# Local and pooled attention with two feed-forward layers on one core: pooled q and k of two pairs of heads as matrix products

## The chip, the cores and the metric

One core of a Trainium2 chip runs the whole program. The metric is the device time of one execution in microseconds (us); the kernel before was run three times, and its median is the figure that changes are compared with.

## The reference

q, k and v are (4, 8, 576, 64): four batches, eight heads, 576 rows. Each head does two attentions and adds them: one on rows averaged by fours (144 pooled rows, its output repeated four times), one on a band of rows less than four apart. Two feed-forward layers follow on all 2304 rows.

```python
q_d = q.reshape(B, H, Sd, factor, D).mean(axis=3)      # factor 4, Sd = 144; k and v alike
out_up = np.repeat(sm_attn(q_d, k_d, v_d), factor, axis=2)
mask = np.abs(pos[:, None] - pos[None, :]) < factor
out_local = softmax(where(mask, scale * q @ k.T, -1e9)) @ v
x = (out_up + out_local), heads side by side: (2304, 512)
h = x @ w_in;  x = (h * sigmoid(h)) @ w_out            # first layer, d_ff = 2048
r = max(x @ w2_in, 0);  out = (s * r * r + b) @ w2_out # second layer
```

## The kernel before

The kernel writes down operations with an engine, a cost, the buffers that they read and write, and a priority (`op`). A planner (`Weave.plan`) walks through them in a modelled time: of the operations that could start first it takes the one with the lowest priority number, gives it to its engine, and so fixes each engine's order. If nothing of high urgency can start on an engine at that moment, the planner puts other work there, such as the splitting of weights. Each engine then executes its own order strictly in that order; the chip's real times change nothing in it. Constants such as `PT0` or `DEC0` are the priorities of the stages. Some operations may go to ScalarE or VectorE (`EITHER`), whichever the planner expects to end first. Where TensorE would idle for more than 0.477 us in the plan at the start, `fill` puts small products on `spin` there.

Heads are worked in pairs, `hq` 0 to 3, so that two heads of 64 fill 128 partitions. For batch 0 the rows of a pair arrive as `nq`, `nk` (96 rows x 6 x 128) and `nv` (`rows`). `b_turn` (L699) transposes q and k by TensorE into `pq`, and copies them to `qkT` (or `qT`, `kT`). `down` does the pooled attention: `pool_rows` adds v by fours (L586, L587), two VectorE reductions (L604, L605) add the turned q and k by fours into `dq` and `dk`, `part` copies `dq` with a factor into the block-diagonal `q_diag`, and then scores `pS` (L634), softmax (L638 to L649, L332), transposes `pT` and the product with v, `pU`, give `upT`. `banded` does the local attention of the pair: `pB` (L748), mask `be` (L756), softmax (L771 to L764), `pBT`, `pBO`, and the sum of both attentions into `xf` (L797).

When a pair's 512 columns of `xf` are done, `x_split` makes `xh` on ScalarE (L541) and the rest `xl` on VectorE (L542). The first layer (`mix1`) multiplies in three products, high by high, low by high, high by low (all at L807), for 16 slices `m` of the weights: `hp`, then `g` (silu, L826), `gh` (L827), `gl` (L828), then `y`. `g` has one buffer and `hp` two: the `hp` of slice m needs `g` of slice m-2, and `g` of slice m needs `gl` of slice m-1. Each block of 512 columns passes through all 16 slices; block 0 starts when the fourth `xl` of batch 0 is there.

Weights arrive as 64-bit numbers and are split on VectorE in four steps a tile: L387, L390, L393, then a cast (L322, either engine) and L397. Both halves stay in SBUF slots of kind `w` for all five blocks: 32 of `NW` = 35 slots once all slices are split. The raw weights and the `nq`, `nk` and `nv` of later batches pass through the others. In batches 2 and 3 the local attention runs on VectorE (`local`, L466 to L528).

Of the kernel before, what the change touches and what calls it, by code (L numbers as in the profile page):

```python
# [8 lines left out]
F32 = mybir.dt.float32  # L9
# [4 lines left out]
ALU = mybir.AluOpType  # L14
AX = mybir.AxisListType

P = 128
# [20 lines left out]
START = 0.56  # L38
TURN = 0.07
FLIGHT = 4  # L40
NW = 35
NACT, NACTV = 1, 0
NNAT, NVW = 10, 4
AHEAD, AHEAD2 = 6, 4
# [34 lines left out]
class Weave:  # L79
# [9 lines left out]
    def op(self, eng, cost, fn, w=(), r=(), pr=0.0, table=None):  # L89
        n, deps = len(self.ops), set()  # L90
        r = [x if isinstance(x, tuple) else (x, None) for x in r]
        w = [x if isinstance(x, tuple) else (x, None) for x in w]

        def hits(d, k):
            return [v for kk, v in d.items() if k is None or kk is None or kk == k]

        for b, k in r:
            deps.update(hits(b.wr, k))
        for b, k in w:
            deps.update(hits(b.wr, k))  # L100
            for v in hits(b.rd, k):
                deps.update(v)
        for b, k in r:
            b.rd.setdefault(k, []).append(n)
        for b, k in w:
            if k is None:
                b.wr, b.rd = {}, {}
            else:
                b.rd.pop(k, None)
            b.wr[k] = n  # L110
        deps.discard(n)
        bufs = []
        for b, _ in r + w:
            if b not in bufs:
                bufs.append(b)
                if not b.left and b.kind in self.turns:
                    self.turns[b.kind].append(b)
                b.left += 1
        self.ops.append((eng if isinstance(eng, tuple) else (eng,), cost, fn, sorted(deps), bufs, pr, table))
        return n  # L120
# [133 lines left out]
def dve(n, c=1):  # L254
    return c * 0.07 + n / 960.0
# [6 lines left out]
def slow(ps):  # L262
    return 1.25 if ps == "ps_first" else 1.0
# [7 lines left out]
def kernel(ctx, tc, q, k, v, w1_in, w1_out, w2_in, w2_out, s2, b2, cst, out):  # L271
    nc = tc.nc
    B, H, S, D = q.shape
# [4 lines left out]
    SD = S // 4  # L278
# [3 lines left out]
    cp = ctx.enter_context(tc.tile_pool(name="cp", bufs=1))  # L282
# [23 lines left out]
    op = W.op  # L306
# [6 lines left out]
    def fixed(pool, shape, dtype, name):  # L313
        b = Buf(None, shape, dtype, name)
        b.tile, b.slot = pool.tile(shape, dtype, name=name), Slot(None, None)
        return b
# [22 lines left out]
    csb = fixed(cp, [P, P], F32, "csb")  # L339
    edge = fixed(cp, [P, 2 * NM], F32, "edge")  # L340
    band = fixed(cp, [P, BW], F32, "band")
    sbt = fixed(cp, [P, 2], F32, "sbt")
    ident = csb[:, 0:P]
    mask_l = edge.tile[:, 0:NM].rearrange("p (s o) -> p s o", o=WIN)
# [4 lines left out]
    op("sp", (1, 0.1), lambda: dma(edge.tile, by_chunk), w=[edge], pr=20)  # L349

    fixed(cp, [P, 16], F32, "pad")
    idle = Buf("g", [P, P], BF16, "idle")
    spin = Buf("y3", [P, 64], F32, "spin")
    op("dve", 0.1, lambda: nc.vector.memset(idle[:], 0.0), w=[idle], pr=-200)
# [194 lines left out]
    nat = {}  # L551
# [12 lines left out]
    CT = 96  # L564
    NCT = S // CT
# [17 lines left out]
    def pool_rows(b, i, pr):  # L583

        t = nat[b, i, "v"]
        op("dve", dve(8 * D), lambda: nc.vector.tensor_tensor(out=t[:, :, :, 0:2], in0=t[:, :, :, 0:2], in1=t[:, :, :, 2:4], op=ALU.add), w=[t], pr=pr)  # L586
        op("dve", dve(4 * D), lambda: nc.vector.tensor_tensor(out=t[:, :, :, 0], in0=t[:, :, :, 0], in1=t[:, :, :, 1], op=ALU.add), w=[t], pr=pr)  # L587
# [8 lines left out]
    def down(b, i, pr, ps="ps"):  # L596
        qd, kd = q_diag[i % 2], Buf("dk", [P, SD], F32, "dk")
        plain = (b, i) in bq
        if plain:
            pool_rows(b, i, pr)  # L600
            (q_, qi), (k_, ki) = bq[b, i], bk[b, i]
            dq = Buf("dk", [P, SD], F32, "dq")
            four = lambda t, i: t[:, i].rearrange("p (n r) -> p n r", r=4)
            op("dve", dve(S), lambda: nc.vector.tensor_reduce(out=dq[:], in_=four(q_, qi), axis=AX.X, op=ALU.add), w=[dq], r=[(q_, (qi, e)) for e in range(2)], pr=pr)  # L604
            op("dve", dve(S), lambda: nc.vector.tensor_reduce(out=kd[:], in_=four(k_, ki), axis=AX.X, op=ALU.add), w=[kd], r=[(k_, (ki, e)) for e in range(2)], pr=pr)  # L605
            src, by, pt = lambda: dq[:], 1.0 / 16.0, None
            source = dq
        else:
            pt = Buf(ps, [P, 2, SD], F32, "pd")
            sums = {nm: pool(b, i, nm, pr) for nm in "qkv"}  # L610
            for j, nm in enumerate("qk"):
                def turned(j=j, nm=nm):
                    for t in range(2):
                        nc.tensor.transpose(pt[:, j, t * QP:(t + 1) * QP], sums[nm](t), ident[:QP, :QP])

                op("pe", 0.12, turned, w=[(pt, j)] + ([kd] if j else [(qd, 0), (qd, 1)]), r=[nat[b, i, nm], csb], pr=pr)
            src, by = lambda: pt[:, 0], -1.0 / 128.0
            source = (pt, 0)
# [9 lines left out]
        e = Buf("de", [DHB, 3, SD], F32, "de")  # L628
# [11 lines left out]
        def norm(eng):  # L640
# [7 lines left out]
           w=[(st, 2)], pr=pr)  # L648
# [260 lines left out]
    for j, (c0, n) in enumerate(blocks):  # L909
        t = Buf("xf", [P, KD, n], F32, "yt")  # L910
# [3 lines left out]
        for kk in range(KD):  # L914
            op("act", act(n), lambda kk=kk, t=t, yh=yh: nc.scalar.copy(out=yh[:, kk], in_=t[:, kk]), w=[(yh, kk)], r=[t], pr=-4)
            op("dve", dve(n), lambda kk=kk, t=t, yh=yh, yl=yl: nc.vector.tensor_tensor(
                out=yl[:, kk], in0=t[:, kk], in1=yh[:, kk].bitcast(F32), op=ALU.subtract), w=[(yl, kk)], r=[t, (yh, kk)], pr=-4)
        nt = n // P
        os_ = [Buf(f"y{d}", [P, DM], F32, f"o{d}") for d in range(nt)]
        for m in range(KF):  # L920
            wi, wo = wts[2, m]
            hp = Buf("h", [P, n], F32, "hp2")
            for kk in range(KD):
# [3 lines left out]
            r = Buf("r2", [P, n], F32, "r2")  # L927
# [6 lines left out]
               w=[gh], r=[r, sbt], pr=-5)  # L934
# [71 lines left out]
```

## Time and profile before

| what | value |
|---|---|
| median of three runs | 930.99 us (929.22 to 931.83) |
| the profiled execution, its own time | 927.62 us |
| its span, first to last instruction | 925.8 us |
| granted TensorE clock, mean over the span | 0.998 |
| busy: TensorE, VectorE, ScalarE | 97%, 64%, 44% |

Durations and idle times come from the profiled execution alone. An instruction's duration in the trace overlaps the next one's start on the same engine, so the price of one more instruction in a full queue is the distance between two starts. The idle time stands in brackets with what ended it. TensorE's share of 97% hides that VectorE is full during the first 75 us, where the first layer's weights are split beside the attention of batch 0.

### The profile page before, as it was taken

Reading aid. Unit: us, or ns where it says so; the run is one execution under the profiler, and the core shown is the slowest. Engines: PE = TensorE matmul, PEld = TensorE weight load, DVE = VectorE, ACT = ScalarE, POOL = GpSimd, SP = SyncE. Lnnn points to the kernel's source line nnn. Section 1 sums busy time; section 2 is a strip of 40 time slices with the busy share of each in tenths; the row PEclk is TensorE's granted clock in tenths of the full one; section 3 lists DMA queues with packets and bytes.
Section 4 is the critical chain, followed back from the end, with each engine's and each line's share of the span. In section 5 each row is a group of like instructions: output and inputs, shape, how many; then the busy total and the mean of one; then the engine's idle time right before and its main releaser. Section 6 shows DMA issues by size and latency. Waiting matters only on the chain.

```text
span 925.8 us, 13309 instructions
## 1 busy us (share of the span) xinstructions
PE 897.2 (97%) x5112; PEld 734.7 (79%) x5112; DVE 594.1 (64%) x1137; ACT 408.1 (44%) x893; POOL 0.2 (0%) x4
## 2 busy tenths in 40 slices
PE   7889999999999999999999999999999999999997
PEld 6667777777778777878889988888888888888896
DVE  6999798699999999881159997432242224222332
ACT  5966878666466322532244543332232224222322
POOL 0000000000000000000000000000000000000000
PEclk9999999999999999999999999999999999999999
DMA  9999202553434211210059540020011000100100
GB/s 195 263 284 270 81 18 64 146 149 80 100 86 124 83 45 54 68 47 1 1 188 335 199 166 1 2 90 1 1 46 46 0 1 23 46 1 0 29 18 24
DMA packets 97530, 78.10 MB, mean 84 GB/s; under 512 B 61500, under 2 KB 83642, under 8 KB 97466
## 3 DMA queue, kind: packets, MB, share of 16 engines
q1 hardware_dynamic: 97154, 76.95, 29.1%
q8 instruction: 40, 0.66, 0.3%
q10 hardware_dynamic: 312, 0.30, 0.1%
q14 instruction: 24, 0.20, 0.1%
HBM read 67.79 MB, written 9.44 MB: 83 GB/s over the span
## 4 chain that ended last, share of the span: by engine, by line
PE 62%; DVE 25%; DMA 5%; SPq 3%; issue 3%; ACT 2%; DVEq 0%; ACTq 0%
PE hp L807 28%; PE o L807 21%; PE y L807 10%; DVE tmp L466 3%; DVE tmp L503 3%; DVE sc L469 3%; SPq L335 3%; DVE gl L828 3%; DVE tmp L508 2%; DMA wo_raw<-in_moe_w_out_dram 1%; DVE tmp L509 1%; DMA nv<-in_v_dram 1%; DVE f L390 1%; DVE f L393 1%; DVE xf L528 1%
## 5 line engine op out<-in xcount | busy, mean ns | idle before, releaser
L807 PE MATMUL hp<-xh,wi 128*128 128x512 f32 (+1 forms) x640 | 201.8, 379 | 3.2 <-ACT g L826 2.7
L807 PE MATMUL y<-gh,wo 128*128 128x512 f32 (+1 forms) x640 | 199.4, 376 | 0.0
L807 PE MATMUL hp<-yh,wi 128*128 128x512 f32 (+1 forms) x640 | 185.8, 368 | 0.0
L807 PE MATMUL o<-wo,gh 128*128 128x512 f32 x576 | 177.5, 389 | 0.0
L935 DVE SCALAR_TENSOR_TENSOR gl<-r,sbt,gh 128x512 fp32r<-128x512 f32 (+1 forms) x80 | 55.8, 697 | 152.5 <-ACT gh L933 152.2
L807 PEld LDWEIGHTS hp<-xh,wi 128*128 128x128 f32 x640 | 116.9, 188 | 26.2 <-ACT g L826 4.9
L807 PEld LDWEIGHTS y<-gh,wo 128*128 128x128 f32 x640 | 117.2, 189 | 19.5 <-issue 0.2
L807 PEld LDWEIGHTS hp<-yh,wi 128*128 128x128 f32 x640 | 116.5, 189 | 20.2
L807 PEld LDWEIGHTS o<-wo,gh 128*128 128x128 f32 x576 | 107.7, 188 | 22.0
L933 ACT ACTIVATE gh<-r,sbt 128x512 fp32r<-128x512 f32 (+1 forms) x80 | 54.5, 682 | 159.5 <-PE o L807 151.4
L807 PE MATMUL hp<-xl,wi 128*128 128x512 f32 (+1 forms) x320 | 118.3, 370 | 1.0 <-DVE xl L542 1.0
L807 PE MATMUL y<-gl,wo 128*128 128x512 f32 (+1 forms) x320 | 118.6, 371 | 0.6 <-DVE gl L828 0.6
L807 PE MATMUL hp<-yl,wi 128*128 128x512 f32 (+1 forms) x320 | 117.7, 368 | 0.0
L807 PE MATMUL o<-wo,gl 128*128 128x512 f32 x288 | 112.0, 389 | 0.0
L931 DVE SCALAR_TENSOR_TENSOR r<-r,sbt 128x512 f32<-128x512 f32 (+1 forms) x80 | 55.8, 698 | 52.1 <-ACT r L930 51.9
L827 ACT CAST gh<-g 128x512 fp32r<-128x512 f32 (+1 forms) x80 | 46.1, 577 | 96.2 <-PE y L807 95.1
L828 DVE TENSOR_TENSOR gl<-g,gh 128x512 fp32r<-128x512 f32 (+1 forms) x80 | 50.4, 630 | 50.3 <-ACT gh L827 50.3
L930 ACT ACTIVATE r<-hp 128x512 f32<-128x512 f32 (+1 forms) x80 | 44.5, 556 | 63.0 <-DVE gl L935 43.9
L807 PEld LDWEIGHTS y<-gl,wo 128*128 128x128 f32 x320 | 60.5, 189 | 10.6 <-DVE gl L828 2.0
L807 PEld LDWEIGHTS hp<-yl,wi 128*128 128x128 f32 x320 | 60.4, 189 | 10.0
L807 PEld LDWEIGHTS hp<-xl,wi 128*128 128x128 f32 x320 | 60.5, 189 | 9.7 <-DVE xl L542 1.6
L826 ACT ACTIVATE g<-hp 128x512 f32<-128x512 f32 (+1 forms) x80 | 44.5, 556 | 50.5 <-DVE gl L828 47.3
(122 smaller groups left out, 986.3 us busy)
## 6 DMA issues: line engine op xcount, KB each, us to landing
wi_raw<-in_moe_w_in_dram SPq DMA_DIRECT2D x32, 512.0 KB
wo_raw<-in_moe_w_out_dram SPq DMA_DIRECT2D x32, 512.0 KB
nq<-in_q_dram SPq DMA_DIRECT2D x32, 144.0 KB
nk<-in_k_dram SPq DMA_DIRECT2D x32, 144.0 KB
nv<-in_v_dram SPq DMA_DIRECT2D x30, 144.0 KB
yd<-ys SPq DMA_DIRECT2D x16, 256.0 KB
yt<-yd SPq DMA_DIRECT2D x4, 1024.0 KB
lk<-in_k_dram SPq DMA_DIRECT2D x6, 384.0 KB
```

The source lines that it names most:

```text
L335: (eng or nc.sync).dma_start(out=out, in_=in_, **kw)
L466: op("dve", dve(n * WIN * D), lambda t=t, i0=i0, n=n, h2=h2: nc.vector.tensor_tensor(out=t[:], in0=wide(qs[:, h2, i0:i0 + n, :].unsqueeze( ...
L469: op("dve", dve(n * WIN * D), lambda t=t, i0=i0, n=n, h2=h2: nc.vector.tensor_reduce(out=sc[:, h2, i0:i0 + n, :], in_=t[:], axis=AX.X, op= ...
L503: op("dve", dve(n * WIN * D), lambda t=t, i0=i0, n=n, h2=h2: nc.vector.tensor_tensor(out=t[:], in0=wide(e[:, h2 * ns + i0:h2 * ns + i0 + n ...
L807: nc.tensor.matmul(t(), lhsT=lhs(i), rhs=rhs(i), start=(first and i == 0), stop=(last and i == 2))
L826: op("act", act(n), lambda g=g, hp=hp: nc.scalar.activation(out=g[:], in_=hp[:], func=AF.Silu), w=[g], r=[hp], pr=-5, table="silu")
L827: op("act", act(n), lambda g=g, gh=gh: nc.scalar.copy(out=gh[:], in_=g[:]), w=[gh], r=[g], pr=-5)
L828: op("dve", dve(n), lambda g=g, gh=gh, gl=gl: nc.vector.tensor_tensor(out=gl[:], in0=g[:], in1=gh[:].bitcast(F32), op=ALU.subtract), w=[gl ...
L930: op("act", act(n), lambda r=r, hp=hp: nc.scalar.activation(out=r[:], in_=hp[:], func=AF.Relu), w=[r], r=[hp], pr=-5)
L931: op("dve", dve(n) + 0.07, lambda r=r: nc.vector.scalar_tensor_tensor(out=r[:], in0=r[:], scalar=sbt[:, 0:1], in1=r[:], op0=ALU.mult, op1= ...
L933: op("act", act(n) + 0.1, lambda r=r, gh=gh: nc.scalar.activation(out=gh[:], in_=r[:], func=AF.Identity, bias=sbt[:, 1:2]), w=[gh], r=[r, ...
L935: op("dve", dve(n) + 0.07, lambda r=r, gh=gh, gl=gl: nc.vector.scalar_tensor_tensor(out=gl[:], in0=r[:], scalar=sbt[:, 1:2], in1=gh[:].bit ...
```

## The change

For batch 0 and pairs 2 and 3, `dq` and `dk` are no longer summed on VectorE from the turned q and k. TensorE multiplies the untransposed rows (six slices of 96 rows x 128) with a 96 x 24 matrix `four` that has ones where a row belongs to a group of four; the result, in PSUM (`pd`), is at once pooled and transposed. `dk` gets a copy from `pd`, and `q_diag` is filled from `pd`. `four` is made once, by one VectorE reduction of the identity. The number of `w` slots goes from 35 to 34, and a padding tile from 16 to 56 floats.

```diff
-NW = 35
+NW = 34
...
+    four = fixed(cp, [96, 24], F32, "four")
...
-    fixed(cp, [P, 16], F32, "pad")
+    op("dve", 0.2, lambda: nc.vector.tensor_reduce(out=four.tile, in_=csb[:96, 0:96].rearrange("p (n r) -> p n r", r=4), axis=AX.X, op=ALU.add), w=[four], r=[csb], pr=-3.2)
+    fixed(cp, [P, 56], F32, "pad")
...
     def down(b, i, pr, ps="ps"):
         qd, kd = q_diag[i % 2], Buf("dk", [P, SD], F32, "dk")
         plain = (b, i) in bq
-        if plain:
+        if plain and b == 0 and i >= 2:
+            pool_rows(b, i, pr)
+            pt = Buf(ps, [P, 2, SD], F32, "pd")
+            for j, nm in enumerate("qk"):
+                def summed(j=j, nm=nm):
+                    for c in range(NCT):
+                        nc.tensor.matmul(pt[:, j, c * CT // 4:(c + 1) * CT // 4], lhsT=nat[b, i, nm][:, c], rhs=four.tile)
+
+                op("pe", 1.2 * slow(ps), summed, w=[(pt, j)] + ([kd] if j else [(qd, 0), (qd, 1)]), r=[nat[b, i, nm], four], pr=pr)
+            src, by = lambda: pt[:, 0], -1.0 / 128.0
+            source = (pt, 0)
+        elif plain:
             pool_rows(b, i, pr)
...
```

Since the planner makes the order, the change moves instructions on every engine. Lines of the changed kernel are higher by 3 up to `down` and by 14 behind it. Three places follow.

VectorE, where pair 2's v is pooled (`nv`) and pair 0's softmax ends (`dst`, `de`). Before:

```order
L604 TENSOR_REDUCE dq<-qkT 128x144
L649 RECIPROCAL dst<-dst 96x3
L587 TENSOR_TENSOR nv<-nv 72x4x64
L332 TENSOR_SCALAR de<-de,dst 96x144 x3
L756 TENSOR_TENSOR be<-pB,band 128x72
L756 TENSOR_TENSOR be<-pB,band 128x216
L605 TENSOR_REDUCE dk<-qkT 128x144
```

With the change:

```order
L590 TENSOR_TENSOR nv<-nv 72x4x64
L663 RECIPROCAL dst<-dst 96x3
L332 TENSOR_SCALAR de<-de,dst 96x144 x3
L390 TENSOR_SCALAR f_413<-wi_raw 128x512
L393 SCALAR_TENSOR_TENSOR f_413<-wi_raw,f_413 128x512
L396 SCALAR_TENSOR_TENSOR f_413<-wi_raw,f_413 128x512
L390 TENSOR_SCALAR f_443<-wo_raw 128x512
L770 TENSOR_TENSOR be<-pB,band 128x72
```

The two reductions are gone, and splitting steps of the first weights (`f`) stand ahead of the mask of pair 1. Counted up to the fourth `xl`, 29 splitting steps stood ahead of it (8 of L387, 7 of L390, 7 of L393, 7 of L397) and 40 stand there now (11, 10, 10, 9); four reductions of 128x576 are gone.

VectorE around the fourth `xl`. Before:

```order
L397 TENSOR_TENSOR wi<-f_930,wi 128x512
L387 TENSOR_SCALAR f_973<-wo_raw 128x512
L542 TENSOR_TENSOR xl<-xf,xh 128x512
L390 SCALAR_TENSOR_TENSOR f_973<-wo_raw,f_973 128x512
L387 TENSOR_SCALAR f_1067<-wi_raw 128x512
L393 SCALAR_TENSOR_TENSOR f_973<-wo_raw,f_973 128x512
```

With the change:

```order
L400 TENSOR_TENSOR wi<-f_933,wi 128x512
L811 TENSOR_TENSOR xf<-pBO,upT 128x256
L396 SCALAR_TENSOR_TENSOR f_960<-wo_raw,f_960 128x512
L390 TENSOR_SCALAR f_983<-wi_raw 128x512
L545 TENSOR_TENSOR xl<-xf,xh 128x512
L400 TENSOR_TENSOR wo<-f_960,wo 128x512
```

The last splitting step of the `wo` tile that ScalarE casts next (`f_973` before, `f_960` now) stood behind the fourth `xl` and stands ahead of it now. On ScalarE both programs have the fourth `xh`, that cast, the loading of the silu table and the first `g`, one behind the other.

SP's queue, the first pairs of batch 2. Before:

```order
L335 DMA nq<-in_q_dram 72x8x64 x2
L335 DMA nk<-in_k_dram 72x8x64 x2
L335 DMA nv<-in_v_dram 72x8x64 x2
L335 DMA lk<-in_k_dram 128x1x768 x2
L335 DMA lv<-in_v_dram 128x1x768 x2
```

With the change:

```order
L335 DMA nq<-in_q_dram 72x8x64 x2
L335 DMA nk<-in_k_dram 72x8x64 x2
L335 DMA lk<-in_k_dram 128x1x768 x2
L335 DMA lv<-in_v_dram 128x1x768 x2
L335 DMA nv<-in_v_dram 72x8x64 x2
```

With two spare slots in place of three, a pair's `nv` is issued apart from its `nq` and `nk`, when one of their slots is free.

## Rows read from the trace of the kernel before

**Rows 1.** The page, its first part: busy time, share and instructions of each engine.

```profile
PE 897.2 (97%) x5112; PEld 734.7 (79%) x5112; DVE 594.1 (64%) x1137; ACT 408.1 (44%) x893; POOL 0.2 (0%) x4
```

**Rows 2.** Busy time by stretch: length; PE, PEld, DVE, ACT, POOL; clock, DMA, GB/s.

```profile
0.00:18.02 18.02, 12.99 (x231) 11.56 (x233) 10.27 (x27) 9.37 (x37) 0.20 (x4) 1.00 0.94 195
18.02:54.57 36.55, 29.99 (x446) 22.72 (x442) 36.27 (x99) 28.87 (x110) 0.00 (x0) 1.00 1.01 275
...
59.41:75.00 15.59, 15.31 (x77) 11.91 (x78) 15.56 (x35) 12.99 (x23) 0.00 (x0) 1.00 0.97 255
75.00:160.00 85.00, 82.29 (x603) 61.62 (x604) 76.41 (x192) 62.72 (x173) 0.00 (x0) 1.00 0.35 94
160.00:500.00 340.00, 334.70 (x1715) 269.96 (x1711) 269.33 (x485) 152.81 (x311) 0.00 (x0) 1.00 0.33 95
```

**Rows 3.** Timeline of TensorE, first block's start: start, us, what [idle before].

```profile
59.41 0.50 PE L807 MATMUL hp<-xh,wi 128*128 128x512 f32 x1 [2.68 <-ACT g L826]
...
62.05 0.62 PE L807 MATMUL hp<-xh,wi 128*128 128x512 f32 x2
62.51 0.39 PE L807 MATMUL hp<-xl,wi 128*128 128x512 f32 x1
```

**Rows 4.** Timeline of ScalarE, the same stretch.

```profile
56.83 0.62 ACT L322 CAST wo<-f 128x512 fp32r<-128x512 f32 x1 [2.46 <-DMA vw<-in_v_dram]
...
58.76 0.60 ACT L826 ACTIVATE g<-hp 128x512 f32<-128x512 f32 x1
...
61.34 0.60 ACT L826 ACTIVATE g<-hp 128x512 f32<-128x512 f32 x1 [1.33 <-DVE gl L828]
```

**Rows 5.** Timeline of VectorE, from the start to the first gl.

```profile
5.34 0.69 DVE L586 TENSOR_TENSOR nv<-nv 72x512 f32<-72x512 f32 x1 [3.80 <-DMA nv<-in_v_dram]
...
18.70 0.74 DVE L604 TENSOR_REDUCE dq<-qkT 128x144 f32<-128x576 f32 x1
19.36 0.16 DVE L649 RECIPROCAL dst<-dst 96x3 f32<-96x3 f32 x1
...
54.57 0.68 DVE L542 TENSOR_TENSOR xl<-xf,xh 128x512 fp32r<-128x512 f32 x1
55.17 0.68 DVE L390 SCALAR_TENSOR_TENSOR f<-wo_raw,f 128x512 int32<-128x512 int32 x1
55.78 0.42 DVE L387 TENSOR_SCALAR f<-wi_raw 128x512 int32<-128x512 int32 x1
56.11 0.68 DVE L393 SCALAR_TENSOR_TENSOR f<-wo_raw,f 128x512 int32<-128x512 int32 x1
...
60.56 0.69 DVE L828 TENSOR_TENSOR gl<-g,gh 128x512 fp32r<-128x512 f32 x1
```

**Rows 6.** Timeline of TensorE: scores, transposes and banded scores of the first pairs.

```profile
10.92 0.72 PE L748 MATMUL pB<-qkT 64*64 64x72 f32 x16
...
12.29 0.90 PE L634 MATMUL pS<-dk,q_diag 128*96 128x144 f32 x6
14.79 0.69 PE L699 MATMUL pq<-csb,nq 96*128 96x96 f32 x6 [1.61 <-DMA vw<-in_v_dram]
```

**Rows 7.** Timeline of TensorE, attention work between products of the first layer.

```profile
66.37 0.41 PE L699 MATMUL pq<-csb,nq 96*128 96x96 f32 x3
66.75 0.50 PE L807 MATMUL hp<-xh,wi 128*128 128x512 f32 x1
67.09 0.40 PE L807 MATMUL hp<-xl,wi 128*128 128x512 f32 x1
```

**Rows 8.** Timeline of VectorE: last local sum of block 2, and its split.

```profile
264.64 0.97 DVE L528 TENSOR_TENSOR xf<-pt,upT 128x128 f32<-128x128 f32 x3
...
282.27 2.48 DVE L542 TENSOR_TENSOR xl<-xf,xh 128x512 fp32r<-128x512 f32 x4
```

**Rows 9.** Timeline of SP's queue: pair 1 of batch 2, its q.

```profile
174.76 1.72 SPq L335 DMA_DIRECT2D nq<-in_q_dram  x2
```

**Rows 10.** Timeline of VectorE: the same q, when it is pooled.

```profile
181.63 0.69 DVE L592 TENSOR_TENSOR nq<-nq 72x512 f32<-72x512 f32 x1 [0.61 <-DMA nq<-in_q_dram]
```

More of the change, by code (lines that the diff above doesn't have):

```diff
@@ L602, in down @@
             dq = Buf("dk", [P, SD], F32, "dq")
-            four = lambda t, i: t[:, i].rearrange("p (n r) -> p n r", r=4)
-            op("dve", dve(S), lambda: nc.vector.tensor_reduce(out=dq[:], in_=four(q_, qi), axis=AX.X, op=ALU.add), w=[dq], r=[(q_, (qi, e)) for e in range(2)], pr=pr)
-            op("dve", dve(S), lambda: nc.vector.tensor_reduce(out=kd[:], in_=four(k_, ki), axis=AX.X, op=ALU.add), w=[kd], r=[(k_, (ki, e)) for e in range(2)], pr=pr)
+            by4 = lambda t, i: t[:, i].rearrange("p (n r) -> p n r", r=4)
+            op("dve", dve(S), lambda: nc.vector.tensor_reduce(out=dq[:], in_=by4(q_, qi), axis=AX.X, op=ALU.add), w=[dq], r=[(q_, (qi, e)) for e in range(2)], pr=pr)
+            op("dve", dve(S), lambda: nc.vector.tensor_reduce(out=kd[:], in_=by4(k_, ki), axis=AX.X, op=ALU.add), w=[kd], r=[(k_, (ki, e)) for e in range(2)], pr=pr)
             src, by, pt = lambda: dq[:], 1.0 / 16.0, None
```

## The prediction

> **What bounds the kernel now.** I read the busy shares first: TensorE 97% of the span, VectorE 64%, ScalarE 44% [rows 1]. So the end is set by how early TensorE gets steady work and by what it waits for later. The table by stretches shows where the rest lies [rows 2]. Up to 54.57 us TensorE is busy 12.99 of 18.02 and 29.99 of 36.55: 11.6 us are free. From 59.41 to 75 it is busy 15.31 of 15.59, from 75 to 160 it lacks 2.71, from 160 to 500 it lacks 5.30. The engine to look at ahead of 54.57 is VectorE: 36.27 of 36.55, in 99 instructions, with the transfers as full (DMA share 1.01). Its queue is in order, so the fourth `xl`, at 54.57 [rows 5], comes when the steps that stand ahead of it are done, whatever they are. Then three things follow each other. TensorE finishes `hp` of the first two slices, and waits 2.68 us for `g` until 59.41 [rows 3]. ScalarE had a cast of `wo` at 56.83, for which VectorE's L393 at 56.11 had to end (the trace names a transfer, but L393 ends at 56.79, just ahead of the cast), then the table load, and `g` at 58.76 [rows 4, 5]. VectorE reaches the first `gl` at 60.56, the second `g` starts at 61.34, and `hp` of the fourth slice at 62.05 [rows 3 to 5]. From there TensorE hardly waits; what it loses up to there nothing gives back but the few waits behind.
>
> **What is removed and added on VectorE ahead of the fourth xl.** One reduction costs 19.36 - 18.70 = 0.66 us of a full queue [rows 5]. Four go: 2.64 us. The copies change little: `q_diag` and `kT` take some 0.8 more, `upT` and one `be` 0.7 less, at 0.2 to 0.4 each by the order; I count 0. The one reduction for `four` stands ahead of the first `nv`, in an idle of 3.80 us [rows 5]: 0, and at most 0.66 if that cover were gone. The splits are the large term. Eleven more of them stand ahead of the fourth `xl`: 3 of L387 at 56.11 - 55.78 = 0.33, 3 of L390 at 55.78 - 55.17 = 0.61, 3 of L393 and 2 of L397, which I take at the 0.60 that `xl` over the same 128x512 takes (55.17 - 54.57) [rows 5]. Sum 0.99 + 1.83 + 3.00 = 5.82 us. Net +3.2: the fourth `xl` at 57.8. The reductions were taken off a full queue, and the queue filled with work that nobody waits for yet. That VectorE could not start that work (a tile not landed) would make it later still, not earlier.
>
> **The products on TensorE.** 24 products of 96x128 with 24 columns; a float32 product leaves two records, as `pS` shows (three products, 6 records) [rows 6]. 48 records: at least 0.72 / 16 = 0.045 each (`pB`, a quarter of the array), at most 0.90 / 6 = 0.15 (`pS`), nearest 0.69 / 6 = 0.115 (`pq`, which loads the same 96x128 slices as weights). Sum 5.5 us, between 2.2 and 7.2. I cost it at 0: it lies beside the full VectorE, in the 11.6 us that TensorE has free. If it falls where TensorE is waited for, a product set of 1.4 us is the price of one such place; that goes into the range. Some 40 `spin` fillers of this stretch go with it; the granted clock of 1.00 [rows 2], the upper level of 2.4 GHz, I take as kept.
>
> Here a rule speaks against the change. A transpose in this trace takes one record, a float32 product two [rows 6]. The Trainium skill (Perfetto Trace Analysis, Optimizing Tensor Performance, Transposes) says that a logical transpose should be a transpose, not a standard matmul, since the transpose skips the arithmetic. By that rule the new step is the dearer way, and if all of it lay on the path the sum below would rise by the products' whole price; with TensorE idle for longer than that, the trace makes it free.
>
> **The restart.** With the change, the splitting step that ScalarE's cast waits for ends ahead of the fourth `xl`, at about 57.8 - 0.33 = 57.5. Cast and table load take 58.76 - 56.83 = 1.93, `g` 0.6 [rows 4]: `g` ends near 60.1 and TensorE goes on there, 0.7 later than at 59.41. So 2.5 of the 3.2 us would be saved. But the first `gl` stands as many steps behind the fourth `xl` as before, 60.56 - 54.57 = 6.0 us [rows 5], now at 63.8. `hp` of the fourth slice follows 62.05 - 60.56 = 1.5 later [rows 3, 5], at 65.3, 3.2 behind. In that gap TensorE does two groups of transposes that it did later before, at 66.75 - 66.37 = 0.38 each [rows 7]. Net **+2.4 us**. What is late next is this chain `gl`, `g`, `hp`; what it queues up behind is VectorE alone.
>
> **The order behind it.** Products of the first layer are interrupted 108 times in the changed order, 99 before. The product behind an interruption takes 67.09 - 66.75 = 0.34 to the next start [rows 7], an undisturbed one (62.51 - 62.05) / 2 = 0.23 [rows 3]. Nine times 0.11: **+1.0 us**. Between 75 and 160 splits that are further ahead could save at most the 2.71 us of waits; I take 0, as VectorE has no less to do there in all. The lost slot I cost at 0, covered by the lead of block 2: its last local sum ended at 264.64 + 0.97, its split came at 282.27 [rows 8], 16.7 us later.
>
> **Sum.** +2.4 + 1.0 = +3.4 us. The profiled execution took 927.62 us, 3.37 less than the median of the three, so it would become 931.0; against the median of 930.99 I predict **934.4 us**. A measurement of this kernel can tell about 0.3%, 2.8 us, from no change.
>
> **Rivals.**
> 1. *The waits absorb it* (no change). The restart costs only the 0.7 us of `g`, because `hp` of the fourth slice finds enough other products ahead of it, or the 2.4 come back in the 2.71 us of waits behind 75. For it: the splits done early are work that need not be done later. Against it: TensorE's waits behind 75 are many short ones, spread over the attention of batch 1. 0.7 + 1.0 = +1.7 at the most, 0 at the least; about 931.7.
> 2. *Faster: the reductions were the chain.* The fourth `xl` is reached earlier, because the pooled attention of pairs 2 and 3 no longer waits for turned q and k, and the splits ahead of it run in idle time that VectorE would have had. It decides if the fourth `xl` starts before 54.57. Price: 2.64 for the reductions, and 0.7 of the wait for `g` with them, -3.3: 927.7. Against it: VectorE was idle 0.28 us between 18.02 and 54.57 [rows 2], so there is no idle time to run them in.
> 3. *The slot shortage.* A pair of batch 2 has its `nv` loaded only when a slot of its `nq` or `nk` is free, and the last pair's result is needed by all sums of block 2. A load took 181.63 - 174.76 = 6.9 us from issue to use [rows 9, 10]. In the changed order only 2.6 us of VectorE work (steps priced as above) stand between block 2's last local sum and its split, where 16.4 stood. If one load's length is not covered, TensorE stands still for 6.9 - 2.6 = 4.3, on top of the sum: 938.7. The Trainium skill (Perfetto Trace Analysis, Optimization Strategy) reads equal gaps that repeat on the engine that should be full as a sign that SBUF lacks room for the next tile. By that rule the gaps would come at each pair of batches 2 and 3; the trace before shows TensorE lacking only 5.30 us of 340 with three spare slots [rows 2], and nothing with two.
> 4. *It doesn't do what it says*: the planner's rest is so much the same that neither the start nor the blocks move. The counts of steps exclude this, and I give it nothing of its own.
>
> **How the numbers follow.** My forecast 0.47, of which a fifth ends below +2.8 because a term is smaller; the waits absorb it 0.28; faster 0.13, a little of it within the bound; the slot shortage 0.12. Faster by over 0.3%: 0.11. Within: 0.10 + 0.28 + 0.02 = 0.40. Slower: 0.37 + 0.12 = 0.49. The forecast's own range is 932.0 to 937.2 (one product set on the path, 1.4, and 1.4 more for waits above; the give-back below). For 8 in 10 the range takes in the second case and most of the shortage, and leaves out most of the faster case: 929.2 to 939.0.
>
> **What would show it.** In the profile after: VectorE full from 18 us on; the fourth `xl` near 57.8, the wait for the first `g` shorter than 2.68 us, the first `gl` near 63.8 with a new wait of TensorE for `g` ahead of the fourth slice; 48 records of the products with `four` at 0.1 us; TensorE's first steady stretch 2 to 3 us later, and all of mix one shifted by that. Wrong: a fourth `xl` before 54.6 (second rival), or TensorE's idle time between 160 and 500 far above 5.30 us (third rival).

## The result, and the profile after

The changed kernel takes **937.64 us** (median of three, 937.44 to 939.14) where the kernel before took 930.99: a ratio of 1.0093 (95% interval 1.0075 to 1.0112). The two medians lie 6.65 us apart, which is 0.71%; the ratio would be 8.7 us. So the size is known to some 2 us. In a later session, against 29 executions of before, it took 935.93 against 928.96: 1.0072 (1.0053 to 1.0092), 6.97 us. The forecast was 934.4, 3.4 us more: the sign came, the time lies inside the range, and the size was half of what the medians show, or less. The profiled execution took 937.44 us, 9.8 more than the profiled one of before, which was faster than all three timed ones (927.62 against 929.22 and more). So differences between the two traces come out larger than those of the medians.

The page of the changed kernel, its first part, and under it the table by stretches (columns as in [rows 2]):

```profile
PE 912.5 (98%) x5125; PEld 748.8 (80%) x5125; DVE 598.3 (64%) x1144; ACT 406.7 (43%) x885; POOL 0.2 (0%) x4
```

```profile
0.00:18.02 18.02, 14.63 (x201) 13.70 (x202) 11.25 (x30) 8.44 (x33) 0.20 (x4) 0.85 0.95 200
18.02:54.57 36.55, 34.80 (x343) 30.17 (x344) 30.50 (x86) 26.93 (x106) 0.00 (x0) 0.70 1.03 283
59.41:75.00 15.59, 13.15 (x164) 9.47 (x161) 15.56 (x31) 8.55 (x16) 0.00 (x0) 1.00 0.98 264
75.00:160.00 85.00, 82.17 (x588) 61.44 (x587) 78.15 (x199) 59.05 (x149) 0.00 (x0) 1.00 0.33 85
160.00:500.00 340.00, 334.45 (x1695) 266.91 (x1694) 266.39 (x481) 157.64 (x326) 0.00 (x0) 1.00 0.29 85
```

Against [rows 2] the last two stretches are as they were. The loss lies ahead of 75 us. From 18.02 to 54.57 the granted clock is 0.70, so TensorE went between the levels of 1.2 and 2.4 GHz; it is busy 34.80 us where it was busy 29.99, and VectorE, full before at 36.27, is busy only 30.50. The list of VectorE's waits of the changed kernel up to its fourth `xl` says for what (line, releaser: total, times, longest):

```profile
DVE be L770 <- PE pB L762: 2.8, 3, 1.4
DVE q_diag L326 <- PE pd L608: 1.0, 1, 1.0
DVE xf L811 <- PE pBO L804: 0.5, 1, 0.5
DVE bst L787 <- ACT be L774: 0.5, 2, 0.4
DVE dst L659 <- PE pS L648: 0.5, 1, 0.5
```

Of 5.7 us of waits in all, 4.8 are for TensorE; before there was one wait, of 1.1 us, for a load. Three of the four sets of products, and the transposes beside them, ran at half speed, as TensorE's timeline shows (a set is 12 records; six transposes took 0.69 in [rows 6]):

```profile
14.57 1.19 PE L713 MATMUL pq<-csb,nq 96*128 96x96 f32 x6 [0.41 <-DMA nq<-in_q_dram]
15.56 2.65 PE L608 MATMUL pd<-four,nq 96*128 96x24 f32 x12
...
31.50 2.60 PE L608 MATMUL pd<-four,nk 96*128 96x24 f32 x12
...
36.15 2.64 PE L608 MATMUL pd<-four,nq 96*128 96x24 f32 x12
...
47.15 1.52 PE L608 MATMUL pd<-four,nk 96*128 96x24 f32 x12
```

The start of the first block, on VectorE, then TensorE (compare [rows 5] and [rows 3]):

```profile
64.17 0.68 DVE L545 TENSOR_TENSOR xl<-xf,xh 128x512 fp32r<-128x512 f32 x1
...
70.14 0.68 DVE L842 TENSOR_TENSOR gl<-g,gh 128x512 fp32r<-128x512 f32 x1
```

```profile
66.53 0.50 PE L821 MATMUL hp<-xh,wi 128*128 128x512 f32 x1 [0.22 <-ACT g L840]
...
69.34 0.47 PE L713 MATMUL pq<-csb,nq 96*128 96x96 f32 x3 [1.15 <-DVE be L770]
...
71.86 0.47 PE L713 MATMUL pq<-csb,nq 96*128 96x96 f32 x3 [0.64 <-ACT qkT L324]
```

The fourth `xl` comes 9.6 us later than before, TensorE goes on at 66.53 in place of 59.41 (7.1), from there to 75 us it waits 1.8 more than before (2.11 against 0.28), and behind 75 its waits add up to 0.7 more. That is 9.6 of the 9.8. Told from VectorE's side, 9.6 us are lost by the first `gl` (70.14 against 60.56) and 0.2 behind it.

A second execution of the same kernel, the run `change_again` below, shows the start with another part of the clock lost: 0.81 on the mean from 18.02 to 54.57, but all four sets of products at the upper level. The stretch, then VectorE, then TensorE:

```profile
18.02:54.57 36.55, 34.23 (x355) 28.32 (x356) 35.37 (x98) 29.75 (x114) 0.00 (x0) 0.81 1.05 289
```

```profile
58.80 0.68 DVE L545 TENSOR_TENSOR xl<-xf,xh 128x512 fp32r<-128x512 f32 x1
...
64.76 0.68 DVE L842 TENSOR_TENSOR gl<-g,gh 128x512 fp32r<-128x512 f32 x1
```

```profile
14.75 1.44 PE L608 MATMUL pd<-four,nq 96*128 96x24 f32 x12
...
30.01 1.42 PE L608 MATMUL pd<-four,nk 96*128 96x24 f32 x12
...
61.16 0.50 PE L821 MATMUL hp<-xh,wi 128*128 128x512 f32 x1 [0.20 <-ACT g L840]
...
64.72 0.44 PE L713 MATMUL pq<-csb,nq 96*128 96x96 f32 x3 [1.90 <-DMA nq<-in_q_dram]
64.94 0.69 PE L821 MATMUL hp<-xh,wi 128*128 128x512 f32 x1
```

It took 932.88 us, the fastest of its six, 5.3 more than the profiled execution of before. What was expected of that run:

> The change itself once more, on the chip of the next three kernels, for the spread of its executions over the clock. With the slot back the executions ran at a mean clock of 0.988 to 0.999 and their time fell by 5.2 us for each 0.01 of it. CLOCK: the change's executions lie at 0.982 to 0.990 and follow the same slope, 936 to 939 us; read off at 1.00 they give 930.5 to 932.5.

The executions lay between 932.88 and 937.42 at mean clocks of 0.986 to 0.991, with a median just below the times expected; the value read off at 1.00 was not tested. The two traces have the same order; of the 5.4 us between their fourth `xl`, 4.3 are VectorE's waits for TensorE, 4.8 us in the one and 0.5 in the other. The second lost less of the clock and kept it for the sets of products; which of the two counts more the traces do not show.

### The profile page after: what moved, and what is told of

The parts are those of the page before. It is cut to its first block, busy times and chain, and to the rows that moved or that the text cites. A ratio compares the mean times of both kernels' runs of the same rounds, so it can differ in the third digit from the quotient of the medians.

```text
span 935.6 us, 13330 instructions
## 1 busy us (share of the span) xinstructions
PE 912.5 (98%) x5125; PEld 748.8 (80%) x5125; DVE 598.3 (64%) x1144; ACT 406.7 (43%) x885; POOL 0.2 (0%) x4
## 4 chain that ended last, share of the span: by engine, by line
PE 66%; DVE 24%; ACT 4%; issue 3%; DMA 2%; SPq 1%; DVEq 0%; ACTq 0%
PE hp L821 30%; PE o L821 21%; PE y L821 10%; DVE tmp L506 3%; DVE tmp L469 3%; DVE sc L472 3%; DVE gl L842 2%; DMA nq<-in_q_dram 2%; DVE tmp L511 1%; DVE f L393 1%; DVE tmp L512 1%; DVE f L396 1%; PE pd L608 1%; SPq L335 1%; ACT be L774 1%
## 5 line engine op out<-in xcount | busy, mean ns | idle before, releaser
L821 PEld LDWEIGHTS hp<-yl,wi 128*128 128x128 f32 x320 | 60.3, 189 | 10.1
```

The costliest lines, as they stand in the source:

```text
L821: nc.tensor.matmul(t(), lhsT=lhs(i), rhs=rhs(i), start=(first and i == 0), stop=(last and i == 2))
```

## The experiments

Three theories. **ORDER**: VectorE's queue ahead of the fourth `xl` sets the start, as forecast. **CLOCK** (with PRODUCTS): TensorE at half clock, with the new products in its queue, is what VectorE waits for. **SLOT**: the lost slot costs behind the start. Against SLOT stands PLAN: not the slot, but the one order that the planner makes with it. Each kernel was timed in five rounds beside before on the same chip. The table has the medians, the ratio with its interval, the mean granted clock over the executions of the kernel (before: 0.9925 to 0.9944), and of the profiled execution its own time (before: 927.62), the start of the fourth `xl` (before: 54.57) and the stretch "behind", from the first `gl` to the last instruction (before: 865.3). A profiled execution is one of several and often not near the median: its last three columns belong together, and not to the median.

| kernel | us / before | ratio | clock | profiled | fourth xl | behind |
|---|---|---|---|---|---|---|
| `change_again` | 935.93 / 928.96 | 1.0072 (1.0053 to 1.0092) | 0.9893 | 932.88 | 58.80 | 866.3 |
| `fillers` | 934.73 / 929.09 | 1.0076 (1.0055 to 1.0097) | 0.9937 | 933.72 | 58.44 | 867.5 |
| `no_fillers` | 927.88 / 929.09 | 0.9991 (0.9979 to 1.0003) | 0.9914 | 929.13 | 55.14 | 866.2 |
| `slot_back` | 931.74 / 929.09 | 1.0020 (1.0002 to 1.0038) | 0.9909 | 932.25 | 62.14 | 862.4 |
| `slot_only` | 927.80 / 928.96 | 0.9990 (0.9977 to 1.0004) | 0.9952 | 929.02 | 56.25 | 864.7 |
| `slot_fillers` | 929.71 / 928.96 | 1.0018 (0.9997 to 1.0040) | 0.9936 | 933.55 | 63.47 | 862.3 |
| `cost_03` | 932.21 / 929.09 | 1.0036 (1.0023 to 1.0050) | 0.9921 | 930.79 | 58.97 | 864.0 |
| `slot_cost_04` | 929.43 / 928.96 | 1.0018 (1.0003 to 1.0033) | 0.9913 | 929.16 | 56.93 | 864.4 |
| `cost_04_fillers` | 931.79 / 929.71 | 1.0030 (1.0013 to 1.0047) | 0.9899 | 932.79 | 59.15 | 865.8 |
| `order_alone` | 935.09 / 928.48 | 1.0065 (1.0042 to 1.0088) | 0.9905 | 930.90 | 60.21 | 862.9 |
| `products_twice` | 939.64 / 928.48 | 1.0127 (1.0100 to 1.0154) | 0.9827 | 939.26 | 67.89 | 863.6 |
| `few_products` | 935.45 / 929.71 | 1.0071 (1.0053 to 1.0090) | 0.9878 | 934.46 | 57.86 | 868.9 |
| `few_products_35` | 928.94 / 929.71 | 1.0001 (0.9990 to 1.0013) | 0.9904 | 929.87 | 60.01 | 862.1 |
| `nq_early` | 938.88 / 928.48 | 1.0123 (1.0096 to 1.0151) | 0.9920 | 936.21 | 57.23 | 871.2 |
| `early_35` | 936.72 / 928.48 | 1.0078 (1.0049 to 1.0107) | 0.9905 | 936.93 | 64.18 | 865.0 |
| `cost_11` | 933.45 / 928.40 | 1.0055 (1.0037 to 1.0073) | 0.9902 | 930.30 | 56.75 | 865.1 |
| `cost_11_35` | 932.98 / 928.40 | 1.0052 (1.0034 to 1.0070) | 0.9891 | 932.40 | 59.17 | 864.9 |
| `cost_125` | 938.48 / 928.40 | 1.0112 (1.0093 to 1.0132) | 0.9900 | 935.11 | 60.66 | 866.7 |

### The order alone

`order_alone` is the kernel before, with only the planner's idea of a cost changed, so that it fills VectorE's queue much as in the changed kernel:

```diff
-        op("pe", 0.9 * slow(ps), score, ...
+        op("pe", (0.9 + (3.0 if b == 0 and i >= 2 else 0.0)) * slow(ps), score, ...
```

> The kernel before (35 slots, reductions on VectorE, no product with four), but the planner believes that the scores of pairs 2 and 3 of batch 0 cost 3 us more each. So it puts 41 splitting steps ahead of the fourth xl (29 before, 40 with the change); fillers stay. ORDER (VectorE's queue ahead of the fourth xl sets the start): 3 x 0.33 + 3 x 0.61 + 6 x 0.60 = 6.4 us more on VectorE, fourth xl at 60 to 62, first gl near 67, VectorE idle under 1.5 us between 18 us and the fourth xl, 932.5 to 936. Rival CLOCK ALONE (the order ahead of the fourth xl costs nothing as long as the clock holds): 928 to 930.

VectorE's timeline of that kernel:

```profile
60.21 0.68 DVE L542 TENSOR_TENSOR xl<-xf,xh 128x512 fp32r<-128x512 f32 x1
...
66.21 0.68 DVE L828 TENSOR_TENSOR gl<-g,gh 128x512 fp32r<-128x512 f32 x1
```

Expected 60 to 62. From 18 us to there the list of VectorE's waits is empty, and the median rises by 6.6 us. So VectorE's order alone makes the fourth `xl` late: no product, no lost slot, all fillers in place. That the late start makes the 6.6 us is not shown. The order behind the start is another one too, and the profiled execution, the fastest of six, is only 3.3 us longer than that of before: 5.6 more by the first `gl`, and 2.4 less behind it. What the slower ones lose was not traced. `cost_125` pushes the same way in the changed kernel, with 45 splitting steps ahead of the fourth `xl`:

```diff
-                op("pe", 1.2 * slow(ps), summed, ...
+                op("pe", 1.25 * slow(ps), summed, ...
```

> 34 slots and a cost of 1.25: 45 splitting steps ahead of the fourth xl and 141 interruptions; VectorE has 2.95 us more to do up to the fourth xl than with the change by the durations of the traces. ORDER: fourth xl 3 us later than the change at the same clock (61 to 62 with little lost clock), 937 to 941. If only the rest of the plan decides: as the change, 935 to 937, or better.

Fourth `xl` at 60.66, 1.9 us behind that of `change_again` where 3 were expected, and 938.48, 10.1 above before, as ORDER had it. Here too the start is not all: the profiled execution is 7.5 us longer than that of before, 6.1 of it by the first `gl`.

### The products, doubled and thinned out

```diff
-                    for c in range(NCT):
+                    for c in [*range(NCT), *range(NCT)]:
```

> The change with 35 slots, and every product with four done twice into the same columns (48 products, 96 records instead of 48): 5.5 us more of TensorE at the full clock by the forecast's 0.115 a record. HIDDEN (the forecast's step: the products lie beside the full VectorE and cost 0): as with 35 slots alone, 930 to 933, on the same line of time over clock (5.2 us for 0.01, 926.2 at 1.00). ON THE PATH (VectorE waits for TensorE where the clock has fallen): 934 to 938, VectorE idle for TensorE by 6 us or more ahead of the fourth xl, and the clock lower than 0.991 on the mean.

HIDDEN (the products cost 0 beside a full VectorE) falls. Beside `slot_back` (the same kernel with single products) the ratio to before rises from 1.0020 to 1.0127, some 10 us for 48 more records. VectorE's waits of `products_twice` up to its fourth `xl`, and the set that it waits for most:

```profile
DVE q_diag L326 <- PE pd L608: 3.6, 1, 3.6
DVE be L770 <- PE pB L762: 2.8, 2, 2.3
DVE dat L322 <- PE pT L671: 1.7, 1, 1.7
```

```profile
36.21 5.21 PE L608 MATMUL pd<-four,nq 96*128 96x24 f32 x24
```

At half clock one doubled set is 5.2 us, and VectorE waits 3.6 of them. Thinned out, a set has two products instead of six. It leaves out four of the six slices and takes 72 columns of the identity in place of `four`, so `dq` and `dk` are not the pooled sums:

```diff
-                    for c in range(NCT):
-                        nc.tensor.matmul(pt[:, j, c * CT // 4:(c + 1) * CT // 4], lhsT=nat[b, i, nm][:, c], rhs=four.tile)
+                    for c in range(2):
+                        nc.tensor.matmul(pt[:, j, c * SD // 2:(c + 1) * SD // 2], lhsT=nat[b, i, nm][:, c], rhs=csb[:96, 0:SD // 2])
```

> The change with two products of 72 columns for each set in place of six of 24 (16 records instead of 48; four of the six slices are left out of the sums); the order of all else is the same. ON THE PATH: mean clock 0.992 or more, VectorE idle for TensorE under 1 us ahead of the fourth xl, fourth xl at 57 to 59, 931.5 to 934 (the order's part alone). ORDER AND SLOT ALONE: as the change, 935 to 937.

```profile
31.78 0.59 PE L608 MATMUL pd<-csb,nq 96*128 96x72 f32 x4
```

```profile
57.86 0.68 DVE L545 TENSOR_TENSOR xl<-xf,xh 128x512 fp32r<-128x512 f32 x1
...
63.82 0.69 DVE L842 TENSOR_TENSOR gl<-g,gh 128x512 fp32r<-128x512 f32 x1
```

A set is 0.59 us, VectorE's waits for TensorE are 0.9 us, the fourth `xl` is where the order puts it (57.86), and still the ratio is 1.0071, like the change's: ON THE PATH (931.5 to 934) did not come, ORDER AND SLOT ALONE did. So with 34 slots the products' own cost is small: nothing against `change_again` (1.0072), 2 us against the first measurement (1.0093), and each ratio has an interval of about 0.2% to either side. What is left is the order, ahead of the start and behind it, or the clock, whose mean (0.9878) was no higher; the runs do not part the two. In the profiled execution, 6.8 us longer than that of before, 3.3 are lost by the first `gl` and 3.6 behind it.

> The same with 35 slots. ON THE PATH: 927.5 to 930 (the version with 35 slots and all products took 931.74). Otherwise 931 to 933.

With 35 slots the same thinning takes the ratio from 1.0020 to 1.0001: about 1.8 us, with intervals that overlap, and all of what that version is slower than before. VectorE and TensorE in its trace:

```profile
60.01 0.69 DVE L545 TENSOR_TENSOR xl<-xf,xh 128x512 fp32r<-128x512 f32 x1
...
65.97 0.69 DVE L842 TENSOR_TENSOR gl<-g,gh 128x512 fp32r<-128x512 f32 x1
```

```profile
75.00:160.00 85.00, 83.08 (x624) 61.43 (x624) 76.23 (x196) 62.76 (x170) 0.00 (x0) 1.00 0.36 94
160.00:500.00 340.00, 336.27 (x1697) 270.68 (x1696) 269.20 (x484) 149.73 (x303) 0.00 (x0) 1.00 0.31 92
```

This start is 5.4 us later than before, and the profiled execution, the tenth of twelve by speed, is only 2.3 us longer than that of before; the median is that of before. Behind the first `gl` it takes 3.2 us less, and from 75 to 500 us TensorE lacks 5.65 in place of 8.01. So ORDER holds for the start, and the order behind can give more than half of a late start back.

### The clock and the fillers

`fillers`: 25 `spin` products ahead of pair 1's first `pq`, and 15 ahead of each set:

```diff
                 def summed(j=j, nm=nm):
+                    fill(15)
                     for c in range(NCT):
...
+                    if b == 0 and hq == 1 and nm == "q" and e == 0:
+                        fill(25)
```

> The change with 85 spin fillers put in by hand: 25 ahead of pair 1's first pq, 15 ahead of each of the four product sets; every other instruction stays in its order (40 splitting steps ahead of the fourth xl). Theory CLOCK (the granted clock fell to 0.50 in two stretches up to 46.8 us, and TensorE's work there doubled; the order alone costs what was forecast): clock 1.00 from 6 us on, a product record near 0.12 us instead of 0.22, the fourth xl between 57 and 60 instead of 64.17, time 933.5 to 935.5. Rival ORDER (the eleven splitting steps and what they push back cost all of it, the clock only fills waits): 936.5 to 938.5 whatever the clock does. Rival FILLERS ON THE PATH (they cost their own 2.5 us): clock 1.00 and still 936 to 938.

The clock went up to 0.9937 and the fourth `xl` came at 58.44, as CLOCK had it. The median, 934.73, lies in CLOCK's range too, but beside before the ratio of 1.0076 is no lower than the change's. TensorE's timeline behind the restart:

```profile
65.96 0.44 PE L716 MATMUL pq<-csb,nq 96*128 96x96 f32 x3 [3.49 <-DMA nq<-in_q_dram]
```

What is gained ahead of the fourth `xl` is in part waited away behind it (3.49 us, 1.90 in `change_again`): the first `pq` of batch 1 stands in the middle of the third slice's `hp`, and its load has not landed.

`no_fillers` takes the groups of 15 and 25 from the kernel before:

```diff
-                if begin[i] > FILL0 and ...
+                if begin[i] > FILL0 and not 10.0 < begin[i] < 40.0 and ...
```

> The kernel before without its two groups of fillers of 15 and 25 between 10 and 40 us; the order of all else unchanged. Theory CLOCK, first form (the change lost the clock because these 40 fillers went): clock under 1.00 between 12 and 47 us, fourth xl at 57 to 61, time 934 to 937. Second form (it was the longer wait of TensorE at 9 to 10.5 us and the products themselves): clock stays 1.00, fourth xl at 54.6, time 930.5 to 931.5.

Before loses nothing without its 40 fillers, and neither form of CLOCK has its time. The mean clock hardly moved (0.9914 against 0.9925 for before on that chip); in the profiled execution it fell to 0.91 from 18.02 to 54.57, and the fourth `xl` came 0.6 us later. With the products a lower clock goes with a larger loss. On one chip, executions of before with a clock of 0.988 took 930.3 us on the mean (four), with 0.996 or more 928.3 (five); those of `slot_back` 932.8 at 0.988 (four) and 927.0 at 0.998 and 0.999 (two): 5.8 us in place of 2.1. These of `slot_back` have 35 slots. The clock itself was set in no run, so this is a spread over executions and not a test.

`nq_early` takes the load in question forward; the rest is `fillers`:

```diff
-            rows(b, hq, "qkv", NAT1 + PT1S * hq, "w", [split_end[1, D1 + D1S * hq]])
+            rows(b, hq, "qkv", NAT1 + PT1S * hq, "w", [split_end[1, 3 if b == 1 and hq == 0 else D1 + D1S * hq]])
```

> The run with fillers and 34 slots, with the first loads of batch 1 (nq, nk, nv, vw of pair 0) issued ahead of the last two pairs of weight tiles; up to the fourth xl the order is the same. LOAD (TensorE's wait of 3.49 us for nq at 65.96 is what is lost behind the start): that wait under 0.5 us and 931 to 932.5 instead of 934.73. GL (the fourth slice's hp waits for the first gl, 5.97 us behind the fourth xl, and the load only lies in the same gap): a wait for g in the place of the wait for nq, 933.5 to 935.5.

Inconclusive: neither time came. A wait of 2.25 us stays at the same `pq` (62.81), now put down to VectorE, and the plan behind is another one: the time is 4 us longer. `early_35` is the same with 35 slots:

> The same with 35 slots. If GL holds, as the run with 35 slots and fillers, 928.5 to 930.5; if LOAD holds, 926 to 928 and faster than before.

Neither came: 936.72, with VectorE waiting for TensorE again (be 2.1, q_diag 1.9) ahead of a fourth `xl` at 64.18. The median of `slot_fillers` is 929.71. Their profiled executions, 936.93 and 933.55, differ by 0.7 us up to the first `gl` and by 2.7 behind it, where their plans differ; the rest between the medians is not settled.

### The slot

> The change with 35 slots of kind w instead of 34, and the padding tile of 16. Theories CLOCK and ORDER: the start is as with the change, 936.5 to 938.5. Rival SLOT (the lost slot costs in the later blocks): 931 to 935. The stretch from 160 to 500 us is busy 334.45 of 340 with the change, so I expect at most 0.5 us from the slot.

```diff
-NW = 34
+NW = 35
...
-    fixed(cp, [P, 56], F32, "pad")
+    fixed(cp, [P, 16], F32, "pad")
```

The room is there. Up to 116 us VectorE and ScalarE have the change's order, the fourth `xl` is late as well (62.14), and yet some 5 us come back: SLOT's range, not that of CLOCK and ORDER. The table by stretches of `slot_back`:

```profile
75.00:160.00 85.00, 82.97 (x606) 61.42 (x606) 77.70 (x200) 63.68 (x174) 0.00 (x0) 1.00 0.36 97
160.00:500.00 340.00, 336.16 (x1709) 270.16 (x1706) 267.39 (x481) 148.18 (x300) 0.00 (x0) 1.00 0.31 90
```

Against the change TensorE lacks 2.03 instead of 2.83, and 3.84 instead of 5.55: 2.5 us fewer waits, and fewer also than before's (2.71 and 5.30). But the slot alone, taken from the kernel before (`NW = 34`, padding 80), costs nothing:

> The kernel before with 34 slots instead of 35 (the padding tile takes the room), nothing else changed; up to the fourth xl its order is that of before, behind it the first layer's products are interrupted 140 times instead of 129. SLOT (the lost slot costs behind the start, in the order of loads and of attention steps): start as before, fourth xl at 54.5 to 55.5, 931.5 to 934. Rival: 34 slots are enough, and the slot mattered only together with the products: 928.5 to 930.5.

and fillers (`slot_fillers`, at 929.71 the range of FILLERS ON THE PATH) and thinner products give pairs with the same gap as the change and `slot_back` (0.0058, 0.0070 and 0.0052 between the ratios):

> The change with 35 slots and with the 85 fillers by hand. CLOCK + SLOT add up: clock 0.995 or more in most executions and 926 to 929 us. FILLERS ON THE PATH (their 2.5 us come on top, and the first load of batch 1, issued at 56 to 57.5 us, makes TensorE wait as in the run with fillers and 34 slots): 929.5 to 932.

Either a slot is worth 5 us beside the products, or the plan that comes out with 34 slots is a bad one by chance. `cost_11` and `cost_11_35`, another such pair (the planner's cost of a set 1.1 instead of 1.2), tell:

> The change (34 slots) with the planner's cost of a product set at 1.1 instead of 1.2: 36 splitting steps ahead of the fourth xl instead of 40, but other copies there, so that by the durations of the traces the first gl comes where it came with the change. SLOT (a missing slot costs 4 to 6 us behind the start): 934 to 937, and slower than the next kernel by 0.4 to 0.7%. PLAN (the slot costs only through the one plan of the change): within 0.3% of the next kernel.

> The same with 35 slots; VectorE's order is the same up to its 187th row, behind the start. SLOT: 929 to 932. PLAN: within 0.3% of the kernel above, wherever that lies.

1.0055 and 1.0052: PLAN. A slot has no fixed price of its own; what costs is the order that the planner happens to make behind the start. The column "behind" agrees. The change, `change_again`, `fillers` and `few_products` have one order on VectorE and ScalarE: 865.5, 866.3, 867.5 and 868.9. `slot_back`, `slot_fillers` and `few_products_35` have the other: 862.4, 862.3 and 862.1 (863.6 with doubled products). TensorE's idle time behind 75 us goes with it: 14.8 to 15.4 us in the first four, 11.7 to 11.9 in these three, 14.1 before. It is made of many short waits, most of them for VectorE. Which of its steps make the difference was not taken apart.

### Fewer splitting steps ahead

The planner's cost of a product set is 0.3 (`cost_03`) or 0.4 here instead of 1.2:

> The change with the planner's cost of a product set at 0.3 instead of 1.2: products the same, but the plan now has 33 splitting steps ahead of the fourth xl (30 before, 41 with the change, two casts to wi or wo among these counts) and fillers of 19 and 27 between 10 and 40 us. VectorE ahead of the fourth xl: -2.64 for four reductions, +2.1 for four splitting steps (0.33 + 0.61 + 0.60 + 0.60), -0.5 in all. Theory CLOCK + ORDER: clock 1.00 and fourth xl at 54 to 55.5, time 929.5 to 931.5; if the clock still falls in it, fourth xl at 57 to 61 and 933 to 936. Rival PRODUCTS (the products themselves are on the path, four sets of 1.4 us): 934 to 937 with the clock at 1.00.

The clock fell to 0.86 from 18.02 to 54.57, and the fourth `xl` came at 58.97 as expected for that case, with 3.5 us of VectorE's waits for TensorE behind 18 us; the median, 932.21, is a little under its range.

> The change with 35 slots and the planner's cost of a product set at 0.4: 29 splitting steps ahead of the fourth xl, as many as before (31 with two casts), no fillers between 10 and 55 us, 128 interruptions (129 before). ORDER (the splitting steps ahead of the fourth xl set the start): VectorE has 2.64 us less to do up to there, fourth xl at 52 to 54.5 as far as the clock holds, 924.5 to 928. PRODUCTS or CLOCK (TensorE is what the fourth xl waits for): fourth xl at 56 to 60, VectorE idle ahead of it, 928 to 932. LOAD (the first nq of batch 1 sets the start): fourth xl early, a wait of TensorE for nq of 2 us or more up to 66 us, 927 to 930.

`slot_cost_04` has as many splitting steps ahead of the fourth `xl` as before and four reductions fewer, and still the fourth `xl` comes at 56.93. ORDER's number (52 to 54.5) falls, and that of PRODUCTS or CLOCK comes (56 to 60, 928 to 932). Of the 2.4 us, VectorE waits 1.3, once 1.4 us for TensorE (`be`), and summed over the trace it works 1.1 longer up to there than before, because the planner now gives it steps that ScalarE did (nine normalisations of `de` instead of three, 1.23; copies of `qT` and `kT`, 0.74; other copies). What is taken off VectorE the planner fills again.

> The change with 35 slots and the planner's cost of 0.4, and 55 fillers in two waits of TensorE: 15 ahead of pair 1's first pq, 40 ahead of pair 2's. Without them this order took 929.43 at a mean clock of 0.991, falling by 4.8 us for 0.01. CLOCK: mean clock 0.994 or more and 926.5 to 928.5, level with before or a little faster. If the clock falls all the same: 929 to 931.

The clock fell all the same (0.9899), and the fourth `xl` came 2.2 us later than without the fillers. No version beat the kernel before by more than the measurement can tell.

## Why the prediction was right in sign and wrong in size

1. **VectorE ahead of the fourth xl: right.** In `change_again`, against before, by distances of starts without the waits: the splitting steps cost 6.2 us more (forecast 5.82), the reductions 2.64 less (2.64), all else 0.6 more (0). Net 4.2, and the fourth `xl` is 4.2 later; forecast 3.2. `order_alone`, with the fourth `xl` 5.6 later, shows such a delay without the products.
2. **The restart: mechanism right, "Net +2.4 us" too small.** The first `gl` follows the fourth `xl` by 5.96 us (forecast 6.0), and the wait for the first `g` shrinks from 2.68 to 0.20, as forecast. TensorE goes on at 61.16, 1.75 later than in [rows 3] (forecast 0.7, plus the 1.0 that point 1 was short). The sentence that fails is "In that gap TensorE does two groups of transposes that it did later before". The order puts them into the gap, but they wait themselves: 1.90 for a load in one trace, 1.15 and 0.64 for VectorE and ScalarE in the other. From there to 75 us TensorE waits 1.6 more than before (1.90 against 0.28); with the 1.75 the restart cost 3.4, not 2.4.
3. **"I cost it at 0: it lies beside the full VectorE", with the granted clock of 1.00 "I take as kept": a step that failed, the largest one in the profiled execution.** Over the change's nine executions the mean was 0.982 to 0.991, and in the profiled one 0.70 in the stretch in which I had put the products at 0 beside a full VectorE. Their price was right at the full clock (1.42 to 1.44 for 12 records, 0.12 each; estimate 0.115), but at the lower level it is 2.6 a set, TensorE is free for 5.1 us up to 54.57 and no longer for 11.6, and VectorE waits for it. Between the two traces of the same kernel the fourth `xl` differs by 5.4 us, 4.3 of them by these waits. By the medians it is less: with thinned products the change costs 0 to 2 us less. I had one execution of before, with the clock up throughout, and took it for the rule: the executions of before on later chips lie between 0.988 and 1.000. The Trainium skill (Perfetto Trace Analysis, Optimizing Tensor Performance, Transposes) says that a logical transpose should be a transpose and not a standard matmul. The thinned products, 1.8 us faster with overlapping intervals, fit its sign and not the products' whole price; no run put transposes in their place.
4. **The order behind, +1.0: not what nine interruptions make.** From the first `gl` to the end the change lost 0.2 us in one trace and 1.1 in the other, but 2.3 and 3.6 in `fillers` and `few_products`, which have the same order. `order_alone` has nine interruptions more than before too, as counted in TensorE's records (107 against 98), and takes 2.4 us less there. So their number does not give the price. Where the interruptions and the lost stretch of clock at 65 us part was not measured.
5. **"The lost slot I cost at 0": the step that failed most by the medians.** With the slot back, and VectorE's order the same up to 116 us, three pairs gain 0.5 to 0.7%, 5 to 6.5 us; in their traces the stretch behind the first `gl` is 3 to 7 us shorter. It is not the third rival: TensorE's idle time between 160 and 500 us rose by 0.25 only, and `slot_only` and the pair of `cost_11` cost nothing. What the lost slot did was to bring out another plan behind the same start.
6. The second rival (faster) is refuted by the fourth `xl`; the first by TensorE's waits between 75 and 500 us, which did not shrink (8.0 before, 8.4 after). With 35 slots they did shrink, to 5.9 in `slot_back`: there part of the late start came back, against "nothing gives back".

So 3.4 us were forecast. Against the one profiled execution of before the change cost 5.3 where the product sets kept the clock, with 4.2 lost by the first `gl`, and 9.8 where three of them lost it, with 9.6. The medians, 6.65 and 6.97, lie between. How they divide into start, clock and plan stays open: in either series of the change the profiled execution is the fastest, and no slower one was traced. That the clock falls is not the products' doing alone: `order_alone` has none and ran at 0.9905, before on the same chip at 0.9925. Why it falls was not settled.

## What to carry to other kernels

Taking work off a full in-order queue gains nothing if a planner fills the place with work that nobody waits for: count what stands ahead of the step that is waited for, not what was removed. Work that is "free" beside another engine has two prices, one for each level of TensorE's clock, and must be hidden at the dearer one; look at several executions before taking the clock as kept. When work is moved into a gap, ask of it, too, what it waits for. And where a planner makes the order, compare several plans before a resource gets a price: here the same start with another order behind it differed by 3 us and more.

## What was not expected of the hardware

A record of a product with 24 columns is no cheaper than a transpose with 96: 1.44 us for 12 records against 0.69 for 6 [rows 6], and one of 72 columns (0.59 for 4) takes 0.15, not three times 0.12. The kernel before ran at mean clocks from 0.988 to 1.000 from one execution to the next. And the clock can fall where the start seems over: in `change_again` the products behind TensorE's wait for `nq` took 0.63 us in place of 0.39, until 68.5 us:

```profile
66.70 0.63 PE L821 MATMUL hp<-xl,wi 128*128 128x512 f32 x1
...
68.50 0.39 PE L821 MATMUL hp<-xl,wi 128*128 128x512 f32 x1
```
